# Talking-heads attention on one Trainium2 core: mixing and scoring pairs of groups in plain float32 on four quarters of TensorE's array, in place of float32r passes over split operands

## The chip, the cores and the metric

The kernel runs on one core of one Trainium2 chip. The time is device microseconds of one execution of the whole program, on that core. The kernel before took 1360.62 us (median of three runs, 1354.05 to 1360.71).

## The reference

The program computes attention in which heads are mixed before and after the softmax, and then two MLPs on its output. The change is in the attention.

```python
scores = (1 / sqrt(64)) * q @ k.T                        # (4, 12, 448, 64): batch, heads, rows, head size
scores = einsum('bhij,hg->bgij', scores, w_pre)          # mix the 12 heads
attn = exp(scores - max(scores, -1))
attn = attn / (sum(attn, -1) + 1e-09)
attn = einsum('bhij,hg->bgij', attn, w_post)             # mix the 12 heads again
x = (attn @ v) laid out as (1792, 768), float32
x = elu(x @ w1_in) @ w1_out                              # 768 -> 2048 -> 768
x = relu(x @ w2_in) ** 2 @ w2_out
```

## The kernel before, in words

**Chunks and groups.** The 448 rows of a batch are cut into four chunks (`CHUNKS`, line 21) of 12, 11, 11 and 11 groups of ten rows; with four batches there are 16 chunks and T = 180 groups. A group is the unit of the softmax stage: ten rows times twelve heads, 120 partitions, by 448 columns.

**Scores.** For each chunk a tile `sc` (120 rows of the chunk on partitions, 12 heads, 448 columns) is filled head by head. The product needs more exactness than one float32r pass gives, so queries and keys are split into a high and a low part of type float32r. In the first four chunks (`first_scores`, line 207) two heads lie on the two halves of the array's rows (64 each), three passes per head. From the fifth chunk on (`scores`, line 227) the two parts of a key are stacked on 128 partitions (`split_k`, line 171) and a head takes two passes (lines 235 and 236). ScalarE copies the scores out of PSUM (`keep_scores`, line 316).

**Groups.** `gather` (line 242) is a DMA on SP that reads ten lines of each head, twelve partitions apart, so that ten rows times twelve heads come to lie on 120 partitions. `split` (line 248) cuts them into high and low part (ScalarE casts, GpSimd subtracts). `mix_pre` (line 256) mixes the heads with a 120 by 120 block matrix in three float32r passes (lines 262 to 264). `maxima` (line 267) takes the row maximum on VectorE and the exponential with its sum on ScalarE. `weigh` (line 277) puts 1/sum into the second mixing matrix, on VectorE. `mix_post` (line 296) mixes again and transposes: four plain float32 calls of 112 columns of weights and 120 moving columns (line 304); VectorE copies the result into `at` (line 310).

**Values.** `values` (line 321) multiplies with v when a chunk is complete, in two steps of 24 plain float32 calls each; two heads lie on the two halves of the array's columns (`o`, line 329). The result goes through `xs` (line 340) to DRAM (`xd`, line 347).

**Order.** Each engine runs its instructions in the order of the program text. The loop of line 442 takes one group per step t and does, in this order, the gather for t+9, the score copies of the step before, the split of t+6, the maxima of t+3, `mix_pre` of t+4, the scores that the table `extra` puts there, the copies of step t-1, `mix_post` of t, `values` and `weigh`; loads and splits of queries and keys follow. All DMAs of the stage go through the queue of SP.

**After attention** the MLPs run (`Mlps.run`, line 1044), with three float32r passes per product (lines 743 to 745). `Mlps.plan` (line 686) puts their first loads and splits into the last steps of the attention loop. From line 1044 on the change alters nothing.

Of the kernel before, what the change touches and what calls it, by code (L numbers as in the profile page):

```python
# [52 lines left out]
def attention(tc, dram, psum, qr, kr, vr, w_pre, w_post, diagonal, xd, mlps):  # L53
    nc = tc.nc
    with ExitStack() as ctx:
# [6 lines left out]
        AHEAD, SPLIT, MIX, MAX, QN, LATE = 9, 6, 4, 3, 3, 4  # L62
        WIDE = len(CHUNKS)


        pre = work.tile([120, NR, H], F32, name="pre")
        post = work.tile([120, 3, 41], F32, name="post")
        pre_h = work.tile([120, 120], F32R, name="pre_h")
        pre_l = work.tile([120, 120], F32R, name="pre_l")
        both = work.tile([120, 2, H], F32, name="both")  # L70
        rows = work.tile([120, NR], F32, name="rows")

        odd = work.tile([128, 1], F32, name="odd")
        turns = work.tile([1, 64, 2], F32, name="turns")
        turns_d = dram.tile([1, 128], F32, name="turns_d")

        def spread_turns():
            for a in range(2):
                nc.gpsimd.memset(turns[:, :, a : a + 1], float(a))
            nc.sync.dma_start(out=turns_d, in_=turns.rearrange("o d a -> o (d a)"))  # L80

        def load_odd():
            nc.sync.dma_start(out=odd, in_=turns_d.rearrange("o p -> p o"))

        def load_mixes():
            for i, w in enumerate((w_pre, w_post)):
                nc.sync.dma_start(out=both[:, i, :], in_=w.unsqueeze(0).broadcast_to([NR, H, H]))
            nc.sync.dma_start(out=rows, in_=diagonal)

        def prepare_mixes():  # L90
            shape = [120, NR, H]
            mask = rows.unsqueeze(2).broadcast_to(shape)
            nc.vector.tensor_scalar_mul(both[:, 0, :], both[:, 0, :], 1.0 / 8.0)
            nc.vector.tensor_tensor(pre, both[:, 0:1, :].broadcast_to(shape), mask, ALU.mult)
            for a in range(3):
                shape = [120, NR, 4]
                nc.vector.tensor_tensor(
                    post[:, a, :40].rearrange("p (g r) -> p r g", g=4),
                    both[:, 1:2, 4 * a : 4 * a + 4].broadcast_to(shape), rows.unsqueeze(2).broadcast_to(shape), ALU.mult,
                )  # L100
            flat = pre.rearrange("p r g -> p (r g)")
            nc.vector.tensor_copy(pre_h, flat)
            nc.vector.tensor_tensor(pre_l, flat, pre_h.bitcast(F32), ALU.subtract)
# [6 lines left out]
        T = len(groups)  # L110
        first.append(T)
        last = first[-2] - AHEAD
# [5 lines left out]

        k_room = work.tile([128, 6, S], F32, name="k_room", tag="at", bufs=2)
        q_room = work.tile([128, 2, 2, 3, CH], F32, name="q_room", tag="v", bufs=3)
        k0, q0, kraw, kp, qraw, qp = {}, {}, {}, {}, {}, {}

        def key_tile():
            return early.tile([128, 2, S], F32R, name="kp", bufs=11)

        def query_tile():
            return early.tile([128, QN, CH], F32R, name="qp", bufs=10)

        def first_k(x, y, queues=(nc.sync, nc.sync)):
            for a in range(2):
                src = kr[0, :, (6 * a + x) * S : (6 * a + y) * S].rearrange("d (p j) -> d p j", j=S)
                queues[a].dma_start(out=k_room[64 * a : 64 * a + 64, x:y, :], in_=src)
# [986 lines left out]
```

## Time and profile before

| what | number |
|---|---|
| median of three runs | 1360.62 us |
| the profiled execution, its own time | 1360.35 us |
| its span, first to last instruction | 1358.5 us |
| TensorE: busy, share of the span | 1342.6 us, 99% |
| VectorE, ScalarE, GpSimd: share of the span | 75%, 59%, 23% |
| mean granted clock of TensorE, of full speed | 0.996 |
| DMA: mean rate over the span | 137 GB/s |

The span is that of the one execution that was profiled; the sum of the prediction is made against its own time. PE is TensorE's matmuls, PEld its weight loads, DVE VectorE, ACT ScalarE, POOL GpSimd, SP the engine whose queue issues the DMAs. A busy TensorE is not a TensorE at its peak: the end of each matmul is modelled, and follow-on matmuls overlap.

### The profile page before, as it was taken

The numbers are of one execution on the slowest core, as the hardware profiler recorded it, in microseconds if no ns is written. First come the engines' busy times: TensorE is split into PE (matmuls) and PEld (weight loads), VectorE is DVE, ScalarE is ACT, GpSimd is POOL, SyncE is SP. The second block draws the span as 40 slices with busy tenths as digits, with TensorE's granted clock in tenths as the row PEclk, the third lists the DMA queues.
The fourth block names the chain that finished last, engine by engine and source line by source line (L and its number), as shares of the span: only waits on it lengthen the run. The fifth ranks groups of instructions, "written<-read, shape, count | busy, mean of one in ns | idle before, by whom it ended". The sixth has DMA issues, their size and how long they took to land.

```text
span 1358.5 us, 24527 instructions
## 1 busy us (share of the span) xinstructions
PE 1342.6 (99%) x8640; PEld 1244.4 (92%) x8641; DVE 1016.9 (75%) x2261; ACT 799.9 (59%) x1736; POOL 308.7 (23%) x288
## 2 busy tenths in 40 slices
PE   8999999999999999999989999999999999999998
PEld 5789999999998999998879999999999998999998
DVE  6777777767777799878788899677885548887452
ACT  6788788878867577533344454456665535445332
POOL 3786786877657000000000000000000000000000
PEclk9999999999999999999989999999999999999999
DMA  5655645654535555465666655503212120222131
GB/s 161 191 166 168 203 151 168 198 161 155 187 138 145 179 171 171 142 190 182 196 205 228 206 197 167 174 31 111 71 59 71 52 77 24 71 64 70 42 99 42
DMA packets 130816, 186.12 MB, mean 137 GB/s; under 512 B 25124, under 2 KB 112005, under 8 KB 130693
## 3 DMA queue, kind: packets, MB, share of 16 engines
q1 hardware_dynamic: 130373, 184.01, 42.4%
q8 instruction: 68, 1.11, 0.3%
q10 hardware_dynamic: 320, 0.55, 0.2%
q14 instruction: 55, 0.45, 0.1%
HBM read 109.63 MB, written 36.18 MB: 107 GB/s over the span
## 4 chain that ended last, share of the span: by engine, by line
PE 86%; DVE 7%; DMA 3%; ACT 2%; issue 1%; POOL 1%; SPq 0%; ACTq 0%; DVEq 0%; POOLq 0%
PE ps_post L304 10%; PE ps_mix L744 7%; PE ps_mix L745 7%; PE ps_mix L743 7%; PE ps_pv L330 6%; PE ps_post L743 5%; PE ps_post L744 5%; PE ps_post L745 5%; PE ps_qk L743 5%; PE ps_qk L745 5%; PE ps_qk L744 5%; PE ps_mix L262 3%; PE ps_mix L264 3%; PE ps_mix L263 3%; PE ps_pv L745 2%; PE ps_pv L743 2%
## 5 line engine op out<-in xcount | busy, mean ns | idle before, releaser
L611 ACT CAST wh<-wf 128x384 fp32r<-128x384 f32 (+1 forms) x272 | 133.3, 492 | 220.2 <-DVE wf L570 141.2
L253 POOL TENSOR_TENSOR gl<-graw,gh 120x448 fp32r<-120x448 f32 x177 | 202.6, 1149 | 110.5 <-ACT gh L252 106.9
L618 DVE TENSOR_TENSOR wl<-wf,wh 128x384 fp32r<-128x384 f32 (+1 forms) x272 | 144.1, 531 | 74.9 <-ACT wh L611 73.3
L304 PEld LDWEIGHTS ps_post<-wg,ex 120*112 120x112 f32 x1440 | 172.3, 176 | 14.6 <-ACT at L313 2.5
L304 PE MATMUL ps_post<-wg,ex 120*112 120x120 f32 x1440 | 178.5, 267 | 1.4 <-ACT at L313 1.2
L749 DVE TENSOR_TENSOR rl<-hr,rh 128x896 fp32r<-128x896 f32 x96 | 104.5, 1090 | 54.1 <-ACT rh L748 54.1
L310 DVE COPY at<-ps_post 112x480 f32<-112x480 f32 x160 | 104.6, 654 | 47.2 <-PE ps_post L304 45.7
L274 ACT ACTIVATE ex<-ps_mix,nmax 120x448 f32<-120x448 f32 x180 | 117.8, 654 | 21.6 <-DVE nmax L270 19.4
L252 ACT CAST gh<-graw 120x448 fp32r<-120x448 f32 x180 | 106.2, 590 | 33.8 <-POOL qp L190 11.6
L748 ACT CAST rh<-hr 128x896 fp32r<-128x896 f32 x96 | 90.0, 939 | 50.4 <-PE ps_qk L745 25.1
L270 DVE TENSOR_REDUCE nmax<-ps_mix 120x1 f32<-120x448 f32 x180 | 111.0, 617 | 6.6 <-PE ps_mix L264 6.6
L318 ACT COPY sc<-ps_qk 120x448 f32<-120x448 f32 x170 | 88.0, 550 | 30.4 <-PE ps_qk L236 26.7
L540 ACT ACTIVATE wf<-wd 128x384 f32<-128x384 f32 (+1 forms) x134 | 67.9, 511 | 35.9 <-DMA wd<-w1o 19.1
L743 PE MATMUL ps_mix<-xh,wh 128*128 128x448 f32 x216 | 79.6, 368 | 3.2 <-ACT xh L748 2.6
L262 PE MATMUL ps_mix<-gh,pre_l 120*120 120x448 f32 x180 | 80.9, 450 | 1.2 <-ACT gh L252 1.2
L744 PE MATMUL ps_mix<-xl,wh 128*128 128x448 f32 x216 | 79.1, 366 | 1.0 <-DVE xl L749 1.0
L745 PE MATMUL ps_mix<-xh,wl 128*128 128x448 f32 x216 | 79.1, 366 | 0.0
L330 PE MATMUL ps_pv<-at,v 112*64 112x110 f32 (+2 forms) x1488 | 78.2, 262 | 0.6 <-DVE at L312 0.6
L330 PEld LDWEIGHTS ps_pv<-at,v 112*64 112x64 f32 x1488 | 71.6, 137 | 4.4 <-DVE at L312 0.8
L570 DVE SCALAR_TENSOR_TENSOR wf<-wd,wf 128x384 int32<-128x384 int32 (+1 forms) x134 | 68.4, 515 | 3.8
L568 DVE SCALAR_TENSOR_TENSOR wf<-wd,wf 128x384 int32<-128x384 int32 (+1 forms) x134 | 67.8, 510 | 3.8
L264 PE MATMUL ps_mix<-gl,pre_h 120*120 120x448 f32 x180 | 66.2, 368 | 0.1
(274 smaller groups left out, 3615.3 us busy)
## 6 DMA issues: line engine op xcount, KB each, us to landing
graw<-sc SPq DMA_DIRECT2D x180, 210.0 KB
wd<-w1i SPq DMA_DIRECT2D x32, 384.0 KB
wd<-w1o SPq DMA_DIRECT2D x48, 256.0 KB
wd<-w2i SPq DMA_DIRECT2D x32, 384.0 KB
wf<-w2of SPq DMA_DIRECT2D x48, 192.0 KB
qraw<-qr SPq DMA_DIRECT2D x48, 180.0 KB
wd<-w2o SPq DMA_DIRECT2D x22, 384.0 KB
kraw<-kr SPq DMA_DIRECT2D x36, 224.0 KB
```

Source lines behind the costliest of these rows:

```text
L253: engine.tensor_tensor(lo, x, hi.bitcast(F32), ALU.subtract)
L262: nc.tensor.matmul(p, pre_l, hi, start=True, stop=False)
L264: nc.tensor.matmul(p, pre_h, lo, start=False, stop=True)
L270: nc.vector.tensor_reduce(nmax, p, AX.X, ALU.max, negate=True)
L274: nc.scalar.activation(e, p, AF.Exp, bias=nmax, scale=1.0, accum_out=tot[t // 2][:, t % 2 : t % 2 + 1])
L304: nc.tensor.matmul(p[:, c, :], e[:, c * NJ : (c + 1) * NJ], w, start=True, stop=True)
L330: nc.tensor.matmul(pv[n][o : o + 64, i % 3, :w], vt[b, i // 3][:, jc, g % 6 * D : (g % 6 + 1) * D], at[n][:, jc, g, :w], start=(jc == 0), ...
L611: self.nc.scalar.copy(hi, f)
L618: self.nc.vector.tensor_tensor(lo, self.single.pop(i), hi.bitcast(F32), ALU.subtract)
L743: mm(p, wh, xh, start=first, stop=False)
L744: mm(p, wh, xl, start=False, stop=False)
L745: mm(p, wl, xh, start=False, stop=last)
```

## The change

The attention now works on pairs of groups, T = 90, one pair per step s.

- Queries and keys are neither split nor doubled. `load_k` and `load_q` put six heads on each half of the partitions, in plain float32. `scores(n, p)` computes two heads in four plain float32 calls: heads on the two halves of the rows, the chunk's query rows 0 to 63 and 56 to 119 (`QROWS`) on the two halves of the columns. `sc` has 128 partitions.
- `gather` brings each group as two DMAs of 60 lines, its first five rows to partitions 0 to 59, its last five to 64 to 123. Nothing splits them.
- `mix_pre` mixes with a 60 by 64 matrix, four plain float32 calls on the four quarters: the two halves r of the groups' rows on the two halves of the array's rows, the two groups on those of the columns.
- `maxima` is as before, on tiles of half a group each of both groups, two per step.
- `weigh` makes the weights of both in one product on GpSimd.
- `mix_post` is 32 plain float32 calls per pair, 60 rows, 64 or 48 columns of weights, 60 moving columns.
- `xs` is copied by ScalarE instead of VectorE. AHEAD, MIX and LATE are 4, 2 and 2 pairs; the tables of `values`, `load_v` and `Mlps.plan` are halved to steps of pairs. The warming matmuls between the first score steps are gone.

The core of the diff, with the new functions (most of the removed ones stand in the listing above):

```diff
-        AHEAD, SPLIT, MIX, MAX, QN, LATE = 9, 6, 4, 3, 3, 4
+        AHEAD, MIX, LATE = 4, 2, 2
+        R5, HALF = NR // 2, NR // 2 * H
+        QROWS = (0, 64), (CH - 64, CH)
+        SROWS = 0, 64 + QROWS[1][1] - QROWS[1][0] - HALF
...
-            raw, k = kraw.pop((b, h)), kp[b, h // 2][:, h % 2, :]
-            hi = early.tile([128, S], F32R, name="khi", bufs=1)
-            nc.scalar.activation(hi, raw, AF.Copy, scale=odd)
-            nc.gpsimd.tensor_tensor(k, raw, hi.bitcast(F32), ALU.subtract)
...
+        def scores(n, p, tags=("qk", "qk")):
 
             if p == 0:
+                sc[n] = score[(n + 1) % 2].tile([128, H, S], F32, name="sc", bufs=1)
+            k = kt[chunks[n][0]]
+            out = [bank(psum, tag)[:, :S] for tag in tags]
+            for c, (x, y) in enumerate(QROWS):
                 for a in range(2):
                     o = slice(64 * a, 64 * a + 64)
+                    nc.tensor.matmul(out[a][64 * c : 64 * c + 64], qt[n][o, p, x:y], k[o, p, :], start=True, stop=True)
+            taken.extend((sc[n][:, 6 * a + p, :], out[a]) for a in range(2))
...
+        def gather(s):
+            for t in (2 * s, 2 * s + 1):
+                n, g = groups[t]
+                x = work.tile([128, S], F32, name="graw", bufs=2 * (AHEAD - MIX + 2))
+                for r in range(2):
+                    lines = slice(SROWS[r] + g, SROWS[r] + g + (R5 - 1) * H + 1, H)
+                    nc.sync.dma_start(out=x[64 * r : 64 * r + HALF], in_=sc[n][lines])
+                graw[t] = x
+
+        def mix_pre(s, warm=0):
+            out = [bank(psum, "mix")[:, :S] for _ in range(2)]
+            e = [graw.pop(2 * s + g) for g in range(2)]
+            for r in range(2):
+                o = slice(64 * r, 64 * r + HALF)
+                for g in range(2):
+                    nc.tensor.matmul(out[r][64 * g : 64 * g + 64], pre64[o], e[g][o], start=True, stop=True)
+            mixed[s] = out
...
+        def weigh(s):
+            sums = tot.pop(s)
+            nc.vector.tensor_scalar_add(sums, sums, 1e-9)
+            rec = work.tile([128, 2], F32, name="rec", bufs=3)
+            nc.vector.reciprocal(rec, sums)
+            w = work.tile([128, 2, HALF], F32, name="wg", bufs=3)
+            shape = [128, 2, HALF]
+            nc.gpsimd.tensor_tensor(
+                w, post.rearrange("p g r -> p (g r)").unsqueeze(1).broadcast_to(shape), rec.unsqueeze(2).broadcast_to(shape),
+                ALU.mult,
+            )
+            wg[s] = w
+
+        def mix_post(s):
+            w = wg.pop(s)
+            out = [bank(psum, "post")[:NJ, : JC * 2 * HALF].rearrange("p (c r k) -> p c r k", c=JC, r=2) for _ in range(2)]
+            for r, e in enumerate(ex.pop(s)):
+                for c in range(JC):
+                    for x, y in ((0, 64), (64, NJ)):
+                        for g in range(2):
+                            o = slice(64 * g, 64 * g + HALF)
+                            nc.tensor.matmul(out[g][x:y, c, r], e[o, c * NJ + x : c * NJ + y], w[o, r], start=True, stop=True)
...
-                nc.vector.tensor_copy(x, p)
-                stored.append((t + LATE, o, x))
+                nc.scalar.copy(x, p)
+                stored.append((s + LATE, o, x))
...
+            keep_scores()
+            if s + AHEAD < T:
+                gather(s + AHEAD)
+            if s + MIX < T:
+                mix_pre(s + MIX)
+                maxima(s + MIX)
             for f, a in beside:
+                if f is scores:
+                    if taken:
+                        keep_scores()
                     f(*a)
+            store_x(s)
+            if s < T:
+                mix_post(s)
+                keep_weighed(s > T - 4)
...
+            keep_x(s)
+            if s + 1 < T:
+                weigh(s + 1)
```

How the order moves on TensorE, in the middle of the stage, before: two groups, each with one head of the next chunk's scores (`qk`) beside it.

```order
L262 MATMUL ps_mix<-gh,pre_l 120x448
L263 MATMUL ps_mix<-gh,pre_h 120x448
L264 MATMUL ps_mix<-gl,pre_h 120x448
L235 MATMUL ps_qk<-kp,qp 120x448
L236 MATMUL ps_qk<-kp,qp 120x448
L304 MATMUL ps_post<-wg,ex 112x120 x4
L262 MATMUL ps_mix<-gh,pre_l 120x448
L263 MATMUL ps_mix<-gh,pre_h 120x448
L264 MATMUL ps_mix<-gl,pre_h 120x448
L235 MATMUL ps_qk<-kp,qp 120x448
L236 MATMUL ps_qk<-kp,qp 120x448
L304 MATMUL ps_post<-wg,ex 112x120 x4
```

And after, one pair: the mix (`pre_83` is the tile `pre64`), two heads of scores, and the first half of `mix_post` (the second is the same again).

```order
L176 MATMUL ps_mix<-graw,pre_83 64x448 x4
L150 MATMUL ps_qk<-kt,qt 64x448 x4
L210 MATMUL ps_post<-wg,ex 64x60 x2
L210 MATMUL ps_post<-wg,ex 48x60 x2
L210 MATMUL ps_post<-wg,ex 64x60 x2
L210 MATMUL ps_post<-wg,ex 48x60 x2
L210 MATMUL ps_post<-wg,ex 64x60 x2
L210 MATMUL ps_post<-wg,ex 48x60 x2
L210 MATMUL ps_post<-wg,ex 64x60 x2
L210 MATMUL ps_post<-wg,ex 48x60 x2
```

A pair was six mixing passes and eight calls of `mix_post`; it is now four and 32, each on a quarter.

On SP's queue around the end of the first batch, before:

```order
L245 DMA graw<-sc 120x1x448 x2
L347 DMA xd_62<-xs 128x3x108
L165 DMA kraw<-kr 128x1x448
L199 DMA v<-vr 112x384
L245 DMA graw<-sc 120x1x448
L347 DMA xd_62<-xs 128x3x108
L245 DMA graw<-sc 120x1x448
L199 DMA v<-vr 112x384
```

And after, the same place:

```order
L167 DMA graw<-sc 60x1x448 x4
L254 DMA xd_62<-xs 128x3x108
L136 DMA v<-vr 112x384
L167 DMA graw<-sc 60x1x448 x4
L254 DMA xd_62<-xs 128x3x108
L129 DMA qt<-qr 64x720 x2
L136 DMA v<-vr 112x384
```

Two groups were two gathers of 120 lines on this queue and are now four of 60; key and query loads between them have become fewer.

## Rows read from the trace of the kernel before

**Rows 1.** The page, busy tenths in 40 equal slices of the span, two engines.
```profile
PE   8999999999999999999989999999999999999998
POOL 3786786877657000000000000000000000000000
```

**Rows 2.** Line 304: instructions, duration (min/median/max, ns), first and last start (us).
```profile
L304 PE MATMUL ps_post<-wg,ex x1440: 263/266/357, 26.1 to 437.9; 120*112 120x120 f32 x180
L304 PEld LDWEIGHTS ps_post<-wg,ex x1440: 172/177/180, 25.9 to 437.8; 120*112 120x112 f32 x180
```

**Rows 3.** Busy time by engine from 100 to 400 us, then clock, DMA share, GB/s.
```profile
core 0: us, PE busy (x) PEld busy (x) DVE busy (x) ACT busy (x) POOL busy (x), PEclk, DMA share, GB/s
100.00:400.00 300.00, 300.00 (x2774) 278.21 (x2774) 222.17 (x614) 240.04 (x596) 216.26 (x199) 1.00 0.52 169
```

**Rows 4.** Timeline of TensorE: start (us), length (us), line, tiles, records.
```profile
43.39 0.86 PE L219 MATMUL ps_qk<-kp,qp 64*120 64x448 f32 x6
...
54.02 0.36 PE L263 MATMUL ps_mix<-gh,pre_h 120*120 120x448 f32 x1
54.22 0.36 PE L264 MATMUL ps_mix<-gl,pre_h 120*120 120x448 f32 x1
54.41 0.98 PE L304 MATMUL ps_post<-wg,ex 120*112 120x120 f32 x8
55.33 2.68 PE L330 MATMUL ps_pv<-at,v 112*64 112x120 f32 x48
...
443.34 0.47 PE L743 MATMUL ps_mix<-xh,wh 128*128 128x448 f32 x1
```

**Rows 5.** Groups of instructions, 300 to 420 us: busy us, mean ns, idle before.
```profile
L253 POOL TENSOR_TENSOR gl<-graw,gh 120x448 fp32r<-120x448 f32 x52 | 60.0, 1158 | 41.3 <-ACT gh L252 38.7 <-PE ps_mix L264 1.4 <-PE ps_mix L263 1.0
L274 ACT ACTIVATE ex<-ps_mix,nmax 120x448 f32<-120x448 f32 x54 | 35.1, 649 | 8.9 <-DVE nmax L270 8.1
L270 DVE TENSOR_REDUCE nmax<-ps_mix 120x1 f32<-120x448 f32 x55 | 33.9, 616 | 1.4 <-PE ps_mix L264 1.4
L310 DVE COPY at<-ps_post 112x480 f32<-112x480 f32 x44 | 28.7, 652 | 11.5 <-PE ps_post L304 11.1
L318 ACT COPY sc<-ps_qk 120x448 f32<-120x448 f32 x48 | 24.8, 542 | 8.8 <-PE ps_qk L236 8.7
L274 ACT ACTIVATION_READ_ACCUMULATOR ex<-ps_mix,nmax 120x1 f32 x53 | 11.1, 209 | 0.0
L288 DVE TENSOR_SCALAR tot<-tot 120x1 f32<-120x1 f32 x54 | 5.5, 143 | 0.0
L340 DVE COPY xs<-ps_pv 128x330 f32<-128x330 f32 (+2 forms) x9 | 4.6, 507 | 13.0 <-PE ps_pv L330 13.0
L290 DVE RECIPROCAL rec<-tot 120x2 f32<-120x2 f32 x27 | 4.5, 166 | 0.9
```

**Rows 6.** SP's issues by line as in rows 2, and SP's timeline.
```profile
L245 SPq DMA_DIRECT2D graw<-sc x180: 768/787/1239, 15.5 to 419.1; - x180
L252 ACT CAST gh<-graw x180: 550/580/696, 19.0 to 427.5; 120x448 fp32r<-120x448 f32 x180
...
L199 SPq DMA_DIRECT2D v<-vr x32: 418/541/1200, 31.1 to 363.8; - x32
L347 SPq DMA_DIRECT2D xd<-xs x32: 360/444/499, 67.4 to 444.0; - x32
L165 SPq DMA_DIRECT2D qraw<-qr x48: 577/582/597, 72.1 to 375.0; - x48
L87 SPq DMA_DIRECT2D both<-w_pre x1: 935/935/935, 9.1 to 9.1; - x1
L88 SPq DMA_DIRECT2D rows<-diagonal x1: 507/507/507, 10.9 to 10.9; - x1
...
303.60 0.77 SPq L245 DMA_DIRECT2D graw<-sc  x1
304.47 0.44 SPq L347 DMA_DIRECT2D xd<-xs  x1
308.20 0.79 SPq L245 DMA_DIRECT2D graw<-sc  x1
309.05 0.59 SPq L165 DMA_DIRECT2D qraw<-qr  x1
```

**Rows 7.** Busy time in a stretch with one gather's data alone; columns as rows 3.
```profile
312.50:312.90 0.40, 0.40 (x4) 0.36 (x3) 0.40 (x2) 0.40 (x3) 0.40 (x1) 1.00 0.66 255
```

**Rows 8.** Timelines of ScalarE, TensorE and SP at the start, columns as rows 4.
```profile
5.33 1.28 ACT L161 ACT_TABLE_LOAD   x1 [5.33 <-DMA q_room<-qr]
3.43 3.44 PE L393 MATMUL ps_pv<-idle 128*128 128x512 bf16 x11
15.51 0.83 SPq L245 DMA_DIRECT2D graw<-sc  x1
```

More of the change, by code (lines that the diff above doesn't have):

```diff
@@ L90, in prepare_mixes @@
+        def load_mixes():
+            for r in range(2):
+                at = slice(64 * r, 64 * r + HALF)
+                for i, w in enumerate((w_pre, w_post)):
+                    nc.sync.dma_start(out=both[at, i, :], in_=w.unsqueeze(0).broadcast_to([R5, H, H]))
+                nc.sync.dma_start(out=rows[at], in_=diagonal[HALF * r : HALF * (r + 1), R5 * r : R5 * (r + 1)])
         def prepare_mixes():
-            shape = [120, NR, H]
-            mask = rows.unsqueeze(2).broadcast_to(shape)
@@ L93, in prepare_mixes @@
             nc.vector.tensor_scalar_mul(both[:, 0, :], both[:, 0, :], 1.0 / 8.0)
[L94 to L100, printed above, removed]
@@ L109, in attention @@
             groups += [(n, g) for g in range(CHUNKS[c][1])]
-        T = len(groups)
-        first.append(T)
-        last = first[-2] - AHEAD
+        T = len(groups) // 2
+        first.append(2 * T)
+        N = len(chunks)
         def width(n):
@@ L417, in attention @@
-        for t in range(AHEAD):
-            gather(t)
-        load_odd()
-        prepare_mixes()
-        for p in range(4):
-            first_scores(1, p, (("mix", "mix"), ("mix", "post"), ("post", "pv"), ("qk", "qk"))[p], (act, dve), True)
-        split(0, nc.vector)
-        split(1, nc.vector)
-        mix_pre(0, 5)
-        split(2)
-        split(3)
+        load_k(0, 0, 1, two)
+        load_q(0, 0, 2, two)
+        load_k(0, 1, 2, two)
+        load_k(0, 2, 4)
+        load_q(0, 2, 6)
@@ L428, in attention @@
+        load_k(0, 4, 6)
+        load_mixes()
+        load_q(1)
+        for n in range(2):
+            for p in range(6):
+                scores(n, p, tags[(6 * n + p) % 4])
+                keep_scores((act, dve))
+            if n == 0:
+                prepare_mixes()
+                for s in range(AHEAD):
+                    gather(s)
+        mix_pre(0)
         maxima(0)
-        mix_pre(1, 2)
+        mix_pre(1)
         maxima(1)
-        weigh_first(0)
-        first_scores(1, 4, ("post", "pv"))
@@ L433, in attention @@
-        mix_pre(2, 2)
-        split(4, nc.vector)
-        weigh_first(1)
-        mix_post(0)
-        keep_scores()
-        maxima(2)
-        first_scores(1, 5)
-        mix_pre(3, 2)
-        split(5)
-        for t in range(T + 3):
-            beside = extra.pop(t, ())
-            if t + AHEAD < T:
-                gather(t + AHEAD)
-            keep_scores()
-            if t + SPLIT < T:
-                split(t + SPLIT)
-            if t + MAX < T:
-                maxima(t + MAX)
-            if t + MIX < T:
-                mix_pre(t + MIX)
+        weigh(0)
@@ L683, in two_parts, with plan @@
                 .rearrange("p (k n) -> p k n", k=k) for part in "hl"]
-    def plan(self, put, T, last, work, early, early_ctx, score_ctx):
+    def plan(self, put, T, last, work, early_ctx, score_ctx):
         w = self.weights
```

325 lines of the change are left out of this document (89 added, 236 removed).

## The prediction

> **What bounds the kernel now.** I read the busy rows first. GpSimd works only in the first thirteen fortieths, so attention is the first third of the span, and TensorE is full there as in the rest [rows 1]. `mix_post` runs from 25.9 to 437.8 us in 1440 records [rows 2]; that is 180 groups of four calls, so each plain float32 call leaves two records. 412 us over 180 groups is 2.29 us a group, 4.58 us for two. TensorE was busy for all of 100 to 400 us, the others for 72 to 80% [rows 3]: the stage is as long as TensorE's queue. The MLPs begin at 443.34 us [rows 4], and the change does not touch their 915 us beyond their first loads. So the question is what a pair of groups costs, 90 times.
>
> TensorE's prices stand in its timeline [rows 4]. A split (float32r) pass over 448 columns starts 0.20 us after the last one (54.02, 54.22). Eight plain records of 120 columns take 0.98 us, 0.27 of it the last one's: 0.10 us each, 0.85 ns a column. Two things are already side by side in it: 48 records of `values`, alternating between two halves of the columns, take 2.68 us, 0.105 us for two; and six passes of 64 rows, alternating between two halves of the rows, take 0.86 us, 0.20 us for two.
>
> **The change, per pair, engine by engine.**
>
> *TensorE.* `mix_pre` was six passes (1.2 us), now four plain calls on four quarters: 8 records of 448 columns at 0.85 ns, 0.38 us each, four abreast: 0.76 us. `scores` likewise 0.76 us, 84 times in 90 steps: 0.71. `mix_post` was 16 records (1.64), now 32 calls, 64 records of 60 columns, 0.051 us each, four abreast: 0.82. `values` stays: 32 times 2.6 us over 90 is 0.93. Sum 3.2 us, 3.4 with the 0.1 us of first weights at each change of shape. Four abreast stands in no row, two abreast does in both directions; its bounds are two abreast (5.5 to 5.7 us) and 3.4. I take four, because rows and columns each show it alone.
>
> *A chain across steps.* `mix_post` of step s needs the two banks that VectorE empties after step s-1 (two copies of 0.65 us), and then `weigh` (0.14 + 0.17 us) and the product on GpSimd [rows 5]. The product was on VectorE; on GpSimd 448 columns take 1.15 us, so 120 take something between 0.3 and 1.15; I take 0.4, by its elements. With some 0.3 us of hand-overs, 2.35 us lie between the end of one `mix_post` and the next, and the loop takes at least 3.2 us. A step with `values` is 4.9 us on TensorE anyway. 3.6 steps of 3.2 and 2 of 4.9 per chunk of 5.6 make 3.8 us on average.
>
> *VectorE and ScalarE.* Two maxima (0.62) and two copies (0.65) as before, one `weigh`: 2.85 us; the subtractions and products that went were not on the path. ScalarE: two exponentials (0.65 + 0.21 us), two score copies (0.52) on most steps, and `xs`, moved here from VectorE (0.51, 32 times): 2.9 us; four casts went. GpSimd loses its 1.15 us subtractions. None of the three reaches 3.8 us, and what TensorE saves covers them [rows 5]. So each of these edits costs nothing while a step is longer than 2.9 us.
>
> *SP.* This is where I expect the bound. A gather is now two DMAs of 60 lines; a pair issues four instead of two, 360 in all. The trace has issues of 120 lines only: 0.79 us, with the next DMA 0.85 to 0.87 us after it [rows 6]. A 48-byte load to 120 partitions took 0.94 us and one of 40 bytes 0.51 [rows 6], so bytes do not set it; the ends are 0.51 and 0.94, and I take 0.79, from the row of the same pattern (lines 12 apart). Then 360 gathers, 0.85 apart, are 306 us. Beside them SP issues 32 `v` (0.54), 32 stores of `xd` (0.44), 28 queries and 18 keys (0.58 for the query load) [rows 6], with 0.06 us between: 65 us. 371 us in 90 pairs is **4.12 us a pair**, above TensorE's 3.8. A new wait: at a chunk's end the first gather of the next waits for the last score copies, with loads for later steps queued behind it; those copies are made some three steps before that gather's turn at 4 us a pair, so it costs nothing.
>
> *DMA engines.* While one gather alone was moving, the DMA engines were busy for 0.66 of 16 and moved 255 GB/s [rows 7]: 210 KB in about 0.85 us on ten of them. It reads ten blocks of twelve lines. Half of it reads five blocks. If it keeps five engines busy it takes the same 0.85 us, and four in a row on the same five take 3.4 us; the rest of the stage's transfers (20 MB by the sizes of their tiles, at 255 / 0.66 = 386 GB/s 51 us) adds 0.57: 3.97 us a pair. If it spreads as the whole did it takes 0.42, 2.3 us a pair. Either end lies under SP's, so it does not enter the sum, but it bears on the fast rival.
>
> The Trainium skill ("DMA: Bandwidth & Descriptors", section "Why a DMA increments its semaphore by 16 and not by 1") says that a copy uses the largest number of engines up to 16 that divides the slowest dimension of both its sides, and the lowest-numbered ones. The trace agrees for the whole gather (120 and 10 give 10; 0.66 of 16 is 10.6). By this rule the halves share five engines, and a pair stays at about 4.0 us even with an issue as short as 0.51 us: 0.15 us times 90 under the forecast, an estimated 1312 us.
>
> **The sum.** The first queries land at 5.33 us and the warming matmuls end at 6.9 [rows 8]. Without casts six score steps of 0.76 us follow, then their copies: the first gather at about 12.5 us instead of 15.5 [rows 8]. 12.5 + 371, and 8 us for the MLPs' 17 early loads, stores and flushes on the same queue: 392. A gather's first user came 3.5 us after its issue (15.5 to 19.0) [rows 6, 8]: 395. Behind the last one lie its mix, exponentials, weights, `mix_post` and two `values`: some 10 us, 405. Two servers near 4.1 us jostle; for that I add 3. So attention ends at 408 in place of 443.3: 35 us less. The profiled execution took 1360.35 us (span 1358.5, and 1.85 around it), 0.3 under the median shown, 1360.62. Forecast: **1326 us**.
>
> **Rivals.**
>
> *Quarters run only two abreast* (slower). No row shows four. Then `mix_pre` and `scores` take 1.53, `mix_post` 1.64, and a pair 5.7 us: from a first mix at about 17 us, 90 steps and 8 us of end are 538, 95 later: 1455 us. It decides as soon as a pair on TensorE is over 4.65 us. Against it: both pairings in the trace run at full rate. 0.12.
>
> *TensorE cannot start 64 short records in time.* The densest stretch is 48 in 2.68 us, 0.056 us each [rows 4], bound by their columns; four abreast need 0.013. With 0.026 each `mix_post` takes 1.65 us, the steps 4.0 and 5.7, on average 4.6: no change, about 1360 us. 0.13, half of it inside 0.5%, the rest on both sides.
>
> The Trainium skill ("TensorE: Matmul & The Clock Gate", "Back-to-back issue gap") gives a floor of about 25 ns from start to start for short matmuls. By it `mix_post` takes 1.6 us and the run some 1357 us. No row here has records that short.
>
> *The issue is dearer*, 0.94 us as for the 48-byte load: 360 times 0.15 us more, 54 us: 1380. 0.10.
>
> *The gathers don't bind*: issue near 0.51 us and their data spread. TensorE's chain then sets 3.8 us a pair: 17 + 342 + 8 = 367, 76 less: 1284 us. For it: issue time has no row of this shape. Against: it needs both; ten engines for ten blocks speaks for five. 0.10.
>
> **How the numbers follow.** The forecast keeps 0.55. Its own range, from 4.0 to 4.3 us a pair, is 1312 to 1345. 1283 to 1385 takes in all rivals but the first, and leaves out some 0.15. A measurement here tells 0.5% (6.8 us) from nothing. Faster by more: 0.55 + 0.10 + 0.05 = 0.70; within: 0.09; slower: 0.12 + 0.09 = 0.21.
>
> **What would show it.** Right: SP issuing gathers almost without a gap from 12 us on, about 0.85 us apart; TensorE idle before `mix_pre`, for `graw`, some 0.3 to 0.5 us a pair; first MLP matmul near 408 us. Four abreast: `mix_pre` and `scores` in about 0.9 us each, `mix_post` in about 1.0. Wrong: TensorE full again with `mix_post` above 1.6 us (pace) or `mix_pre` near 1.5 (two abreast); SP idle while TensorE waits for VectorE or GpSimd before `mix_post` (chain); or gathers that land far later than 3.5 us after their issue, so that the engines, not SP, are the queue.

## The result, and the profile after

The changed kernel took 1370.68 us (median of six, 1367.95 to 1376.57), the kernel before, run beside it, 1357.82 (1353.66 to 1361.51). The ratio is 1.0102, 95% interval 1.0069 to 1.0134: **slower by 1%**. The forecast was 1326, faster by 2.5%; 1370.68 lies inside the range and on the wrong side of zero. The profiled execution took 1376.57 us, 5.9 above the median; its span is 1374.8.

The page of the changed kernel, busy tenths in 40 slices, against [rows 1]:

```profile
PE   8899889988888999999989999999999999999998
POOL 0000001000003100000000000000000000000000
```

Three lines of the code, with instructions, duration (min/median/max, ns), first and last start (us): `mix_post` against [rows 2], SyncE's gathers against [rows 6], and the first line of the MLPs against [rows 4].

```profile
L210 PE MATMUL ps_post<-wg,ex x5760: 209/218/358, 25.9 to 451.1; 60*48 60x60 f32 x102, 60*64 60x60 f32 x97
...
L167 SPq DMA_DIRECT2D graw<-sc x360: 720/737/1139, 12.7 to 435.8; - x180
...
L614 PE MATMUL ps_mix<-xh,wh x216: 362/363/742, 459.9 to 1233.5; 128*128 128x448 f32 x108
```

The MLPs start at 459.9 us; before it was 443.34 [rows 4], and 408 was forecast. From there to the end it is 914.9 us, before 915.2. So the whole difference is in the attention, 16.6 us of it in these two executions. The table of runs below gives where the MLPs start in each profiled execution; that execution can lie some us off the median (8 above it in e5 and e13, 5 below in e17), and what follows that start takes 910 to 920 us.

Busy time by stretch, columns as [rows 3]: the middle of the stage, then half a microsecond in which a half gather moved alone.

```profile
100.00:400.00 300.00, 267.44 (x6136) 165.58 (x6128) 162.87 (x383) 153.72 (x411) 24.40 (x63) 0.97 0.46 148
206.50:207.00 0.50, 0.50 (x8) 0.20 (x6) 0.40 (x4) 0.00 (x0) 0.00 (x0) 1.00 0.32 113
```

Every engine is less busy than in [rows 3]: TensorE 267 instead of 300, VectorE 163 instead of 222, ScalarE 154 instead of 240, GpSimd 24 instead of 216. The work went as forecast, and the time did not. No engine is full any more; the time is in waits.

An ordinary step (one pair, one unit of scores, no values), from the timeline of the changed kernel:

```profile
204.27 1.09 PE L210 MATMUL ps_post<-wg,ex 60*64 60x60 f32 x62 [0.69 <-POOL wg L196]
...
205.48 1.22 DVE L225 COPY at<-ps_post 112x480 f32<-112x480 f32 x2 [0.74 <-PE ps_post L210]
...
206.61 0.16 DVE L191 TENSOR_SCALAR tot<-tot 128x2 f32<-128x2 f32 x1
206.88 0.17 DVE L193 RECIPROCAL rec<-tot 128x2 f32<-128x2 f32 x1
...
207.19 0.39 POOL L196 TENSOR_TENSOR wg<-post,rec 128x120 f32<-128x120 f32 x1 [2.98 <-DVE rec L193]
207.63 0.95 PEld L210 LDWEIGHTS ps_post<-wg,ex 60*64 60x64 f32 x62 [0.88 <-POOL wg L196]
```

`mix_post` to `mix_post` takes 3.36 us, by just the chain that the prediction put at 3.2: copies, sum, reciprocal, product (0.39 us, taken as 0.4), next matmul. The 51 steps like it have a median of 3.38 us. With the other steps that hold no second unit of scores, those with `values` among them, 76 in all, the mean is 4.1 us, where the prediction had 3.8 for its chain. Two other places are not like it. Here a step with **two units of scores** (a unit is one call of `scores`, two heads):

```profile
113.06 1.10 PE L210 MATMUL ps_post<-wg,ex 60*64 60x60 f32 x64
...
116.50 0.98 PE L176 MATMUL ps_mix<-graw,pre 60*64 60x448 f32 x8
...
117.30 0.94 PE L150 MATMUL ps_qk<-kt,qt 64*64 64x448 f32 x8
...
118.89 0.62 ACT L186 ACTIVATE ex<-ps_mix,nmax 128x448 f32<-128x448 f32 x1
...
119.50 0.96 ACT L155 COPY sc<-ps_qk 128x448 f32<-128x448 f32 x2
120.08 0.19 PEld L150 LDWEIGHTS ps_qk<-kt,qt 64*64 64x64 f32 x2 [2.61 <-ACT sc L155]
...
121.33 2.35 PE L210 MATMUL ps_post<-wg,ex 60*64 60x60 f32 x57
```

A chunk has six units for five to six steps, so some step takes two. The second waits for ScalarE to empty the banks of the first, and those copies stand behind the exponentials of s+2: 2.61 us. The step takes 8.27 us (113.06 to 121.33); counted over the trace there are 12 like it with `values`, 101.8 us together. Then `mix_post` itself takes 2.35 us for 57 records instead of 1.09 for 62: half the rate. The granted clock of this stretch is 0.50, which is 1.2 GHz (0.97 over the stage, 1.00 before [rows 3]); columns as there:

```profile
121.33:123.70 2.37, 2.37 (x74) 2.08 (x70) 0.00 (x0) 0.97 (x2) 0.00 (x0) 0.50 0.39 129
```

And here the end of a chunk on SyncE's queue, with what it waits for (timelines of three engines):

```profile
162.32 1.19 PE L150 MATMUL ps_qk<-kt,qt 64*64 64x448 f32 x8
164.60 2.13 SPq L120 DMA_DIRECT2D kt<-kr  x2
...
165.04 2.68 PE L237 MATMUL ps_pv<-at,v 112*64 112x120 f32 x48
...
167.77 0.46 ACT L247 COPY xs<-ps_pv 128x360 f32<-128x360 f32 x1 [2.43 <-PE ps_pv L237]
168.12 0.97 ACT L155 COPY sc<-ps_qk 128x448 f32<-128x448 f32 x2
...
169.12 2.48 SPq L167 DMA_DIRECT2D graw<-sc  x3
```

The chunk's last scores are computed at 162.32 and copied at 168.12: their copies stand behind `xs`, which waits for `values`. SyncE (SP) idles from 166.73 to 169.12. Waits of SyncE and of ScalarE in the whole stretch, 100 to 400 us (total, times, longest):

```profile
SPq L167 <- ACT sc L155: 27.1, 10, 4.8
SPq L167 <- PE ps_mix L176: 12.7, 24, 0.9
...
ACT xs L247 <- PE ps_pv L237: 56.1, 22, 7.2
```

Only the first row is a long stall of SyncE; none of the 24 waits in the second lasts over 0.9 us.

### The profile page after: what moved, and what is told of

Its sections match the earlier page's. It is cut to its first block, busy times and chain, and to the rows that moved or that the text cites. A ratio compares the mean times of both kernels' runs of the same rounds, so it can differ in the third digit from the quotient of the medians.

```text
span 1374.8 us, 33357 instructions
## 1 busy us (share of the span) xinstructions
PE 1309.4 (95%) x13456; PEld 1106.4 (80%) x13456; DVE 938.9 (68%) x1946; ACT 683.8 (50%) x1476; POOL 49.5 (4%) x110
## 4 chain that ended last, share of the span: by engine, by line
PE 73%; DVE 11%; DMA 7%; ACT 3%; SPq 2%; issue 2%; POOL 1%; ACTq 0%; DVEq 0%; POOLq 0%
PE ps_mix L615 7%; PE ps_mix L616 7%; PE ps_mix L614 7%; PE ps_post L210 7%; PE ps_pv L237 5%; PE ps_post L615 5%; PE ps_post L616 5%; PE ps_post L614 5%; PE ps_qk L614 5%; DMA graw<-sc 5%; PE ps_qk L615 5%; PE ps_qk L616 5%; PE ps_mix L176 3%; DVE at L225 3%; PE ps_qk L150 3%; PE ps_pv L615 2%
## 5 line engine op out<-in xcount | busy, mean ns | idle before, releaser
L186 ACT ACTIVATE ex<-ps_mix,nmax 128x448 f32<-128x448 f32 x180 | 112.8, 631 | 119.3 <-DVE nmax L184 118.7
L210 PEld LDWEIGHTS ps_post<-wg,ex 60*48 60x48 f32 (+1 forms) x5760 | 113.3, 134 | 70.7 <-POOL wg L196 53.8
L184 DVE TENSOR_REDUCE nmax<-ps_mix 128x1 f32<-128x448 f32 x180 | 104.0, 615 | 70.5 <-PE ps_mix L176 69.0
L150 PE MATMUL ps_qk<-kt,qt 64*64 64x448 f32 x696 | 123.1, 589 | 25.1 <-ACT sc L155 24.4
L210 PE MATMUL ps_post<-wg,ex 60*48 60x60 f32 (+1 forms) x5760 | 123.7, 226 | 17.8 <-POOL wg L196 15.2
L176 PE MATMUL ps_mix<-graw,pre 60*64 60x448 f32 x720 | 120.1, 574 | 8.4 <-DMA graw<-sc 7.5
L150 PEld LDWEIGHTS ps_qk<-kt,qt 64*64 64x64 f32 x696 | 38.4, 139 | 90.9 <-ACT sc L155 80.8
L155 ACT COPY sc<-ps_qk 128x448 f32<-128x448 f32 x171 | 82.8, 541 | 21.5 <-PE ps_qk L150 17.0
L411 ACT ACTIVATE wf<-wd 128x384 f32<-128x384 f32 (+1 forms) x134 | 68.0, 512 | 40.9 <-DMA wd<-w1o 23.9
L237 PE MATMUL ps_pv<-at,v 112*64 112x110 f32 (+2 forms) x1488 | 81.4, 268 | 1.1 <-DVE at L222 1.1
L614 PE MATMUL ps_mix<-wh,rh 128*128 128x384 f32 x176 | 59.1, 336 | 0.0
```

The costliest lines, as they stand in the source:

```text
L150: nc.tensor.matmul(out[a][64 * c : 64 * c + 64], qt[n][o, p, x:y], k[o, p, :], start=True, stop=True)
L176: nc.tensor.matmul(out[r][64 * g : 64 * g + 64], pre64[o], e[g][o], start=True, stop=True)
L186: nc.scalar.activation(e, p, AF.Exp, bias=nmax, scale=1.0, accum_out=tot[s][:, r : r + 1])
L210: nc.tensor.matmul(out[g][x:y, c, r], e[o, c * NJ + x : c * NJ + y], w[o, r], start=True, stop=True)
L237: nc.tensor.matmul(pv[n][o : o + 64, i % 3, :w], vt[b, i // 3][:, jc, g % 6 * D : (g % 6 + 1) * D], at[n][:, jc, g, :w], start=(jc == 0), ...
L614: mm(p, wh, xh, start=first, stop=False)
```

## The experiments

Five readings were to be told apart. **A**: the steps with two units of scores. **B**, later **R**: the gathers' pace, by SyncE's issue or by the five engines. **C**: the chain from `mix_post` to `mix_post`. **D**: the clock after the wait. **S**: score copies behind `xs`. Ratios are to the kernel before, run beside each; the last column is the start of the first MLP matmul in the profiled execution.

| run | median us | ratio, 95% | MLPs start us |
|---|---|---|---|
| changed kernel | 1370.7 | 1.0069 to 1.0134 | 460 |
| e1 second unit late | 1359.0 | 0.9994 to 1.0023 | 447 |
| e2 half the gathers | 1348.4 | 0.9910 to 0.9954 | 434 |
| e3 weights early | 1363.5 | 1.0040 to 1.0085 | 447 |
| e4 TensorE kept busy | 1369.8 | 1.0061 to 1.0108 | 456 |
| e5 = e1 + e3 | 1353.3 | 0.9950 to 0.9988 | 443 |
| e6 = e5 + e2 | 1304.6 | 0.9584 to 0.9642 | 391 |
| e7 = e5, half on GpSimd | 1337.8 | 0.9837 to 0.9887 | 422 |
| e8 = e5, loads on GpSimd | 1359.4 | 0.9994 to 1.0029 | 446 |
| e9 = e5, half the bytes | 1329.4 | 0.9748 to 0.9836 | 417 |
| e10 = e7, later in the step | 1374.7 | 1.0074 to 1.0159 | 459 |
| e11 all on GpSimd | 1394.0 | 1.0220 to 1.0308 | 481 |
| e12 = e7, lead 5 | 1317.3 | 0.9643 to 0.9694 | 400 |
| e13 = e5, lead 5 | 1350.6 | 0.9920 to 0.9964 | 436 |
| e14 lead 5 alone | 1384.8 | 1.0159 to 1.0232 | 467 |
| e15 = e13, third score tile | 1342.9 | 0.9846 to 0.9897 | 429 |
| e16 = e12, third score tile | 1315.6 | 0.9650 to 0.9694 | 400 |
| e17 copies ahead of `xs` | 1361.2 | 1.0001 to 1.0043 | 442 |
| **e18 = e16 + e17** | **1303.6** | 0.9563 to 0.9621 | 388 |

**The second unit behind `mix_post` (A).**

```diff
-            for f, a in beside:
-                if f is scores:
-                    if taken:
-                        keep_scores()
-                    f(*a)
+            units = [a for f, a in beside if f is scores]
+            for a in units[:1]:
+                scores(*a)
...
+            for a in units[1:]:
+                keep_scores()
+                scores(*a)
```

> The second unit of scores of a step is issued behind that step's mix_post and values, instead of ahead of them; nothing else differs from the changed kernel. Theory A (time goes in the steps with two units of scores, whose second unit waits for ScalarE's copies behind the exponentials of s+2, with the clock fall behind it): the 12 steps of 8.24 us come down to about 5 to 5.5 us, the first matmul of the MLPs moves from 459.9 to about 415 to 425 us, and the time falls by 35 to 50 us, to about 1325 to 1335. Theory B (SyncE's issue of gathers or the DMA engines bind, at about 4.1 us a pair as the prediction had it): the wait only moves to the gathers; the time falls by less than 15 us. Theory C (the ordinary step's chain through weigh and GpSimd): the ordinary step stays at 3.36 us here, and the time falls only by what the two-unit steps give.

11.7 us less: under B's 15, and a quarter to a third of the 35 to 50 that A expected. The stall is gone: `mix_post` now comes at once.

```profile
116.78 0.94 PE L150 MATMUL ps_qk<-kt,qt 64*64 64x448 f32 x8
117.53 1.10 PE L210 MATMUL ps_post<-wg,ex 60*64 60x60 f32 x64
```

But TensorE now waits for gathered scores (total, times, longest, 100 to 400 us):

```profile
PEld ps_mix L176 <- DMA graw<-sc: 22.2, 25, 2.3
PE ps_mix L176 <- DMA graw<-sc: 8.0, 10, 1.5
```

In the changed kernel these were

```profile
PEld ps_mix L176 <- DMA graw<-sc: 9.6, 13, 1.5
PE ps_mix L176 <- DMA graw<-sc: 3.2, 6, 0.8
```

so a part of the time won came back as waits for the gathers.

**Half the gathers (B).**

```diff
-                x = work.tile([128, S], F32, name="graw", bufs=2 * (AHEAD - MIX + 2))
-                for r in range(2):
+                if t < 8:
+                    room.append(work.tile([128, S], F32, name=f"graw{t}"))
+                x = room[t % 8]
+                for r in range(2 if t < 8 else 1):
```

> After the first four pairs the second half (r = 1) of each group's gather is left out and the mixing reads old values there: 180 fewer transfers, less about 8, on SyncE's queue, the same matmuls. Theory B (issue and transfers of the gathers bind): at half the issue, 2.1 us a pair, the time falls by 40 us or more. Theory A (the steps with two units of scores bind): the two-unit steps stay near 8 us and the ordinary ones at 3.36; only the direct waits for gathered scores go, 37 us of them in all over the whole run and partly beside other waits, so the time falls by 10 to 25 us.

22.3 us less: inside A's 10 to 25, not B's 40 or more. With the order as it is, half the gathers do not give the forecast.

**The weights early (C).**

```diff
             store_x(s)
+            if s + 1 < T:
+                weigh(s + 1)
             if s < T:
                 mix_post(s)
...
             keep_x(s)
-            if s + 1 < T:
-                weigh(s + 1)
```

> The weights of the next step (sum, reciprocal, GpSimd's product) are issued before mix_post of this step and its copies instead of behind them. Theory C: the 51 ordinary steps lose the part of their chain through VectorE's copies and GpSimd, from 3.36 us to about 2.7 to 3.0, unless the exponentials' chain takes over: 15 to 30 us less in all. Theory A alone: the two-unit steps stay at 8.2 us, and whatever the ordinary steps gain is partly lost again in them; under 10 us less. Theory B: no change, since the gathers set the pace.

7.2 us less. The ordinary step did shorten; its median fell from 3.38 to 3.07 us over 51 steps (`mix_post` starts at 208.43 and 211.41 in one):

```profile
208.43 1.29 PE L210 MATMUL ps_post<-wg,ex 60*64 60x60 f32 x58
...
211.41 1.41 PE L210 MATMUL ps_post<-wg,ex 60*64 60x60 f32 x62
```

C is a real chain. 51 steps of 0.31 us would be 16 us; about half of that was lost elsewhere.

**TensorE kept busy in the wait (D).**

```diff
                     if taken:
                         keep_scores()
+                        for _ in range(2):
+                            nc.tensor.matmul(bank(psum, "post")[:64, :S], pre64, kt[chunks[a[0]][0]][:, 0, :], start=True, stop=True)
```

> Ahead of the second unit of scores of a step two plain float32 matmuls with unused results go into the banks that mix_post is to use, so that TensorE has work in the wait for ScalarE's copies. Theory D (a good part of the loss is the clock, which after that wait halves and makes mix_post 2.35 us instead of 0.93): mix_post of the two-unit steps comes back to about 1 us and the time falls by 10 to 18 us. Theory A without D (the wait itself is the price): the wait stays at about 2 us, the two added matmuls fit into it, and the time moves by less than 5 us.

Within 1 us: D falls.

```profile
119.23 1.72 PE L326 MATMUL ps_post<-kt,pre 128*64 128x448 f32 x4
121.14 1.03 PE L150 MATMUL ps_qk<-kt,qt 64*64 64x448 f32 x5 [0.19 <-ACT sc L155]
...
122.05 1.29 PE L210 MATMUL ps_post<-wg,ex 60*64 60x60 f32 x58
```

The added work fills the wait, `mix_post` is back near its full rate (1.29 us for 58 records), and the granted clock over the stage rises from 0.97 to 0.99. Yet the twelve steps of this kind take 101.3 us together, as against 101.8. The low clock followed the waits, and the time that it took came back as waits when it was gone.

**Both orders, and what stands behind them (R).** e5 has the edits of e1 and e3, e6 also that of e2.

> Both orders together: the second unit of scores behind mix_post and values, and the weights of the next step ahead of mix_post. Each alone gave 11.7 and 7.2 us against the changed kernel's 1370.7. If these are two waits at different steps (theories A and C) they add up: about 1352. Theory R (behind both stands the pace of the gathers: SyncE's issue, 360 of 0.74 to 0.84 us, or the DMA engines): the steps won only run into the waits for gathered scores, the time stays at 1356 to 1360, and the waits of mix_pre for graw grow beyond the 53 us of the first order alone.

> Both orders together, and after the first four pairs the second half of each group's gather left out (the mixing reads old values there). Theory R: without the gathers' pace the two orders show their whole worth, 25 us or more below the same kernel with all its gathers, 1325 or less. Theories A and C without R: within 12 us of the same kernel with all gathers.

e5 is at 1353.3, so the two orders nearly add up, but the other sign of R came too: the waits for `graw` grew, over the whole stage from e1's 53 us to 68, between 100 and 400 us to

```profile
PEld ps_mix L176 <- DMA graw<-sc: 29.4, 36, 2.4
PE ps_mix L176 <- DMA graw<-sc: 7.9, 12, 1.6
```

e6 is at 1304.6, 49 us below e5 and 21 below the forecast: with the other removed, the orders are worth 44 us and the gathers 49, but alone they gave 17 and 22. Two costs of nearly the same size lie side by side; removing one shows the other.

**Issue or transfer?** e7 sends half of the issues to another queue, e9 halves the bytes and keeps every issue.

```diff
-                    nc.sync.dma_start(out=x[64 * r : 64 * r + HALF], in_=sc[n][lines])
+                    (nc.sync, nc.gpsimd)[r].dma_start(out=x[64 * r : 64 * r + HALF], in_=sc[n][lines])    # e7
...
+                w = S if t < 8 else S // 2                                                              # e9
...
+                    nc.sync.dma_start(out=x[64 * r : 64 * r + HALF, :w], in_=sc[n][lines, :, :w])        # e9
```

> Both orders together, and the second half of each group's gather issued from GpSimd's queue instead of SyncE's: the same bytes and engines, half the issues for each queue. If R is SyncE's issue, the time comes down toward that of the kernel with half the gathers, 1325 to 1335. If R is the DMA engines (the five that a half gather uses), it stays within 5 us of the kernel with both orders. If GpSimd's issue is dear or a wait there delays the weights, it is slower than that.

> Both orders together, and after the first four pairs every gather moves only the first 224 of its 448 columns (the mixing reads old values in the others): all 360 issues, half the bytes. It parts the two readings of theory R, which the kernel with half the gathers (1304.6) and the one with half of them on GpSimd's queue (1337.8) leave together. If SyncE's issue is the pace, 4 x 0.74 to 0.84 us a pair as before, the time stays near the 1353 of both orders, at 1343 or more. If the transfers on their engines are the pace, it falls to near 1305. Between the two, both count.

e9 gave 23.9 of the 48.7 us that e6 gave, and 24.8 are left for half the issues at the same bytes: both count, half each. The prediction had transfers under SyncE's term, and so at nothing. e7 gave 15.6, between what its expectation had for the issue and for the engines; GpSimd issues a gather in 0.60 us. It is not a clean test of the issue: which engines carry the transfers of that queue the trace does not tell (the 16 were busy for a mean 0.57 of the stretch in e7, 0.48 in e5).

> Both orders together, and the loads of keys, queries and values after the start issued from GpSimd's queue, so that SyncE issues little but gathers and stores of x. If the loads that SyncE issues between the gathers at the ends of batches make the gathers late, the time falls by 5 to 10 us against both orders alone; if the transfers themselves are what is in the way, by less than 3 us.

6 us slower than e5, which neither expectation allowed for: taking the other loads off SyncE's queue does not help. SyncE's own time fell to 3.49 us a pair here (table below), and its waits for score copies rose from 20.2 us in e5 to 43.5: the pace is not set by SyncE's issue alone. Why the kernel became slower stays open.

**The place on GpSimd's queue.**

> As the kernel with the second halves on GpSimd's queue (1337.8), but these are issued at the end of the step, behind the product of the next weights, so that a gather that waits for ScalarE's copies holds no weights back on GpSimd. If the 49.6 us that GpSimd's gathers wait for the copies delay the weights, the time falls by 5 to 15 us, to 1323 to 1333. If they have slack there, it stays within 3 us, or rises a little since these gathers start later.

> As the last, but all gathers after the first pairs and these too are issued from GpSimd's queue, at the end of the step: SyncE issues no gather at all, GpSimd 360 at 0.61 us, 2.5 us a pair, beside 0.4 us of weights. If GpSimd's queue spreads a transfer over more engines than SyncE's and 2.9 us a pair fit, the time falls toward 1305 to 1325. If GpSimd's own pace or the 4.8 us from its issue to landing binds, it is slower than with half of them there, 1340 or more.

36.9 and 56.2 us slower than e7: the gain that e10's expectation allowed for did not come, and e11 went the way of its slower reading. Waits for gathers in e11 (18.0 and 13.7 us in e7):

```profile
PEld ps_mix L176 <- DMA graw<-sc: 57.1, 52, 4.6
PE ps_mix L176 <- DMA graw<-sc: 27.5, 26, 4.5
```

Issued at the end of the step, gathers come later. That points to the lead rather than to the place on the queue as what e7 lacked, and the next runs lengthen it (`AHEAD` 5 instead of 4).

> As the kernel with both orders and the second halves on GpSimd's queue (1337.8), with every gather one step further ahead of its mixing (five steps instead of four, ten gathered tiles instead of eight), which moves the scores a step forward too. If what is left of the waits for gathered scores (47 us on TensorE's queues in that kernel) is the time from GpSimd's issue to landing, one step more of lead takes 10 us or more off, to 1328 or less. If it is the rate of issue and transfer, a longer lead changes nothing: within 4 us.

20.4 us less than e7, as expected of the lead. And with all gathers on SyncE, with the orders (e13) and without (e14):

> Both orders together, all gathers on SyncE's queue, and five steps of lead instead of four. If the pace of SyncE and the five engines of a gather binds (theory R as a rate), a longer lead changes nothing: within 4 us of 1353.3. If R was only the lead (a gather starts when its chunk's last scores are copied, and its four transfers need over two steps to land), the time falls by 15 us or more, to 1338 or less, as it did where half of the gathers were on GpSimd's queue (1337.8 to 1317.3).

> The changed kernel with five steps of lead instead of four and nothing else. If the lead was what was missing in the first place, the time falls by 15 us or more, to 1356 or less, near the kernel before. If the two-unit steps, the weights' chain and the gathers' rate set it, it stays within 4 us of 1370.7.

e13 gained nothing that the intervals tell apart, e14 lost 14 us. What its trace shows is that ScalarE's copies `xs` wait for `values` for 80.1 us instead of 56.1 and that SyncE's longer gaps are 45 us instead of 36; no run tests whether that is the cause. In e13 the stalls moved: SyncE waits less for copies, and ScalarE's copies wait for the gathers of the chunk but one before, whose score tile they overwrite.

```profile
SPq L167 <- ACT sc L155: 12.8, 4, 6.3
...
ACT sc L155 <- DMA graw<-sc: 15.9, 4, 7.6
```

A third score tile takes that wait away (three pools instead of two, `score[(N - 1 - n) % 3]`).

> Both orders, all gathers on SyncE's queue, five steps of lead, and a third tile of scores, so that ScalarE's copies of a new chunk need not wait for the gathers of the chunk but one before (28 us of such waits between 100 and 400 us with two tiles). If SyncE's own issue, 4.05 to 4.12 us a pair, is the floor and the rest of its 4.5 us a pair were waits that the order and the two tiles make, the attention ends some 25 to 35 us earlier and the time is 1315 to 1330, the forecast's figure. If the five engines' rate is the floor, the waits turn into later landings and the time stays above 1340.

> The fastest kernel so far (both orders, second halves on GpSimd's queue, five steps of lead; 1317.3) with a third tile of scores. There ScalarE's copies wait only 9 us for loads and gathers between 100 and 400 us, so at most 5 to 8 us can go: 1309 to 1317. If it falls by more than 12 us, the two tiles held back more than the waits on them show.

In e15 SyncE's gathers wait for score copies 0.8 us in all. The first row of SyncE's waits is now one behind transfers, and TensorE's waits for gathers, 5.0 and 2.0 us in e13, are back:

```profile
SPq L167 <- DMA graw<-sc: 14.1, 32, 0.9
...
PEld ps_mix L176 <- DMA graw<-sc: 26.5, 33, 2.2
PE ps_mix L176 <- DMA graw<-sc: 8.6, 13, 1.4
```

The MLPs start at 428.9 us instead of 436.3, not 25 to 35 earlier, and the time, 1342.9, is above 1340. Both signs of the second reading came: the waits turned into later landings. SyncE's own issue was not the floor. e16 is as fast as e12 within the intervals.

To see SyncE's share, its DMA issues that start between 100 and 400 us were added up from the traces, and the gaps between the end of one and the start of the next:

| run | gathers | their issue us | other issues us | gaps under 0.2 us | longer gaps us | own time per pair |
|---|---|---|---|---|---|---|
| changed | 256 | 190.9 | 50.5 | 21.4 | 36.1 | 4.11 |
| e5 | 267 | 200.0 | 52.0 | 23.2 | 24.3 | 4.12 |
| e13 | 267 | 198.2 | 49.4 | 22.8 | 29.2 | 4.05 |
| e15 | 273 | 202.5 | 49.3 | 23.0 | 24.9 | 4.03 |
| e9 | 280 | 207.9 | 50.9 | 29.1 | 12.3 | 4.11 |
| e8 | 264 | 199.2 | 13.3 | 18.1 | 69.2 | 3.49 |

A pair is four gathers; the last column is the first three sums over that. In the changed kernel the longer gaps add 36.1 / 64 = 0.56 us to 4.11, and 64 pairs fill the 300 us at 4.69 each. e8, with 3.49 of its own, still takes 4.55; e9, with half the bytes and 4.11, takes 4.29.

**Score copies ahead of `xs` (S).**

```diff
+            keep_scores()
             keep_x(s)
```

> The changed kernel with one call moved: the score copies of a step are issued on ScalarE ahead of the copy of the values (xs) instead of behind it. Theory S: at a chunk's end xs, which the change moved to ScalarE, waits for TensorE's values, the last score copies stand behind it, and SyncE's first gather of the chunk waits for them (10 waits, 27 us, between 100 and 400 us). Then most of these waits go, SyncE comes near its own 4.1 us a pair, and the time falls by 15 to 35 us, to 1336 to 1356. If the step with two units of scores is what makes the copies late, not xs, it falls by less than 8 us.

> The fastest kernel so far (both orders, second halves on GpSimd's queue, five steps of lead, three score tiles; 1315.6) with the same call moved. Its lead already covers the late copies and the gathers on GpSimd wait 8 us for them between 100 and 400 us; so 0 to 6 us less. More would mean that the copies behind xs hold the scores up on TensorE as well.

One line moved, 9.4 us less, between the two figures expected. ScalarE's wait for `values` fell from 56.1 to 36.8 us; SyncE's for the copies, of which most was to go, stayed:

```profile
SPq L167 <- ACT sc L155: 26.6, 10, 5.9
...
ACT xs L247 <- PE ps_pv L237: 36.8, 24, 3.5
```

So S has its price, but the copies behind `xs` are not what makes SyncE's stalls. At the same place in the fastest kernel it gave 12 us: e18, 1303.6 us, ratio 0.9592, **4.1% faster than the kernel before** and about 5% faster than the change as it was. It is twice what was expected there. TensorE's wait for the copies, which the expectation named for that case, fell only from 40.6 to 36.4 us, so where the rest came from stays open.

## Why the prediction was wrong

*Right, by the traces.* Four quarters run abreast: `mix_post` 1.09 us for 62 records (forecast 1.0), `scores` and `mix_pre` 0.94 and 0.98 for eight (0.9). So the slower rival, two abreast, and the one on short records are out, and so is the dearer issue. The ordinary chain 3.36 us (3.2), the product on GpSimd 0.39 (0.4), the gather's issue 0.74 (0.79), the first gather at 12.7 us (12.5). SyncE's own time is 4.11 us a pair; the sum said **4.12**. The time from the MLPs' start to the end did not change.

*Wrong: the step from 4.12 us a pair to 371 us of SyncE without a pause.* The prediction saw the new wait: "at a chunk's end the first gather of the next waits for the last score copies ... those copies are made some three steps before that gather's turn at 4 us a pair, so it costs nothing." The queue cannot be three steps behind: a gather is issued four steps ahead of its pair and mixed two steps ahead, so the lead is two steps, and one of them goes to landing (3.5 us [rows 6, 8]). In the program text the copies stand in the same step as that gather, right ahead of it. In the trace they come after the gather's turn, ten times in 300 us: 27.1 us, all longer gaps together 36.1, 0.56 us a pair. Added up in the same way from the first gather (12.7 us) to the last (435.8), the longer gaps are 54 us. SyncE's issues and short gaps are 370 us there, where the forecast had 371 and 8 for the MLPs' loads. All that the sum had for the 54 was the "3 us" for two servers that jostle. The last gather comes 44 us after the forecast's 392 for that. A smaller term failed too: from the last gather to the MLPs it is 24 us, not 13.5 (landing 3.5, and 10 for one `mix_post` and what goes with it), since four `mix_post` are still to come and the last two steps of `values` take 4.59 and 3.09 us, others 2.48. 44 and 11, less the 3, make the 52 us between 408 and 459.9.

*Why the copies are late* is the second step that failed. "Each of these edits costs nothing while a step is longer than 2.9 us" priced ScalarE by its busy time and averaged the steps. Its order decided: copies behind exponentials in the two-unit steps (8.27 us instead of 3.36), and behind the moved `xs`, which waits for `values`. e1 and e17 each removed one such place and gave 11.7 and 9.4 us; e3 did the like on VectorE, with the weights ahead of the copies, and gave 7.2. None of the three took SyncE's waits for the copies away (24.5, 26.6 and 26.4 us left of 27.1), so which of the late copies makes which stall is not shown one by one.

*The transfers.* "Either end lies under SP's, so it does not enter the sum" also fell: with all issues kept, half the bytes gave 23.9 us (e9). Five engines it is: 0.32 of 16, or 5.1, and 113 GB/s with one half gather in motion, where the whole one had 0.66 and 255 [rows 7]. By the rule in the Trainium skill ("DMA: Bandwidth & Descriptors", "Why a DMA increments its semaphore by 16 and not by 1"), 60 lines out of five blocks go over five engines. The trace agrees. Two servers, 4.11 us a pair measured and 3.97 estimated by the prediction, tied by a lead of two steps, do not run at the larger of the two: even e15, with a step more of lead and without the stalls for copies, took 300 / 68.25 = 4.40 us a pair.

What stays open: what part of e15's last 0.36 us a pair is the transfers, why the longer lead alone (e14) costs 14 us and the loads on GpSimd's queue (e8) 6.

## What to carry to other kernels

A term per resource, summed over the stage, is a floor and not a forecast where two terms lie close together (here 4.12 and 3.97 us a pair) and the lead between them is short: look at the step with the most work and at the instruction that frees the next stage, and ask what stands ahead of it on its engine. When an edit that removes a plain wait gives a quarter to a third of its size, look for a second cost of the same size beside it, and take both away in one run (17 and 22 us alone, 66 together). Copies that feed a queue go ahead of copies that wait for something else; here that was one line.

## What the runs showed of the hardware

The records of short plain float32 matmuls on four quarters start 15 ns apart: in the ordinary step 62 `mix_post` records start from 204.27 us on, and the last two stand in two rows of their own, both at 205.19 us:

```profile
205.19 0.22 PE L210 MATMUL ps_post<-wg,ex 60*64 60x60 f32 x1
```

That is 0.92 us for 63 starts, 15 ns a record, and two records make a call: 29 ns a call. The Trainium skill ("TensorE: Matmul & The Clock Gate", "Back-to-back issue gap") gives about 25 ns as the least from start to start; read by record, as the prediction read it, `mix_post` would take an estimated 1.6 us. The trace does not agree with that reading. By call its 32 starts would take an estimated 0.8 us at least, which the 0.92 us measured allow; no run here has shorter calls that would show the floor itself.

A gather issued from GpSimd's queue takes it 0.60 us, less than SyncE's 0.74, and lands a median 4.8 us after its issue (e7):

```profile
graw<-sc POOLq DMA_DIRECT2D x138, 105.0 KB, 4.8
```

In e11, where GpSimd issues them all, the median is 3.2 us. With half the gathers there, one more step of lead gave 20 us (e12); with all of them on SyncE's queue it gave 3 (e13), and 10 together with the third score tile (e15). The traces hold no landing times for SyncE's queue, so the two cannot be compared.
